# Who gets which 8 KB buffer in the last pass: a store ring of five, and all other buffers for loads

## The chip, the cores and the metric

The kernel runs on one core of a Trainium2 chip. The metric is the device time of one execution in microseconds, the median of several runs. Lower is better.

## The reference, cut to what matters

The reference computes four layers on one token and the gradients of all weights and of both caches by reverse differentiation. Layer A is attention over a cache of 65,536 positions with 32 query heads and 4 key/value heads; layer B is a dense layer with a squared ReLU. Both are used twice, with the same weights and the same cache.

```python
def A(x, k_cache, v_cache, wq, wo):          # Hq=32, Hkv=4, Dh=128, Sk=65536, D=1024
    q = (x @ wq) split into 32 heads
    scores = einsum("bhqd,bhkd->bhqk", q, repeat(k_cache, 8)) * Dh ** -0.5
    p = softmax(scores)
    return einsum("bhqk,bhkd->bhqd", p, repeat(v_cache, 8)) as one row @ wo
def B(x, w1, b1, w2, b2):
    return relu(x @ w1 + b1) ** 2 @ w2 + b2
x = x + A(layernorm(x)); x = x + B(layernorm(x))
x = x + A(layernorm(x)); x = x + B(layernorm(x))
# outputs: x, and the gradients of x, k_cache, v_cache, wq, wo, w1, b1, w2, b2 for a given grad_out
```

K and V caches are 64 MB each in bf16, and so are their two gradients. They make nearly all the traffic.

## The kernel before, in words

**Passes.** The caches don't fit on the chip, so they are read again in each of four passes: the two attention layers forward (`attn_fwd`, twice), the backward pass of the second attention layer (`attn_bwd3`), and the last pass (`attn_bwd4`, line 1263), which finishes the backward pass of the first attention layer and writes the gradients of K and V for both layers together. Dense stages lie between the passes.

**Buffers.** One tile, the arena (line 259), holds 20 buffers of 8 KB per partition, 1 MB each. Eight of them begin the last pass as planes that keep the softmax numerators of both attention layers for the four key/value groups; `E_done` (line 881) gives back the two planes of a group when that group is finished. Seven more begin it with V blocks that the pass before left there, already transposed. Five are free. Every other use takes a buffer by `take_one` (line 283) through `Slot` (line 305) and gives it back through `give_slot` (line 318). Taking and giving happen in the program's order, when the program is written, not at run time. `NOW["step"]` counts the steps of the pipeline, and `FREE` holds for each free buffer the step at which it was given back; a buffer that was handed to a store gets 5 steps added (`STORE_STEPS`, line 67). At run time, whoever overwrites a buffer waits by semaphore until its last use has ended: a matmul that reads it, or the DMA that stores it.

**The last pass.** Blocks are 32 cache rows per partition, 1 MB: 64 K blocks and 64 V blocks. Items are an eighth of a row group (8 columns); there are 256, and a step of `pipeline` (line 825) advances each stage by one. The stages, with their lags, stand in line 1439:

- `vT` (line 1311) loads a V block, transposes it on TensorE (line 1319) and copies it out of PSUM (line 1322); `vS` (line 1339) multiplies it with the output gradients (line 1350) and makes X on VectorE (line 1367).
- `eIn` (line 1325) copies the planes on GpSimd (line 1328); `eT` and `xT` transpose (line 1334) into `xt` (line 1336).
- `dV8` and `dK8` call `outer16` (line 1382), which takes a buffer (line 1385), fills it with the gradient of one half block in two steps (matmuls in line 1390, copies out of PSUM through `evac`, lines 161 on ScalarE and 164 on VectorE) and stores it (line 1396).
- `k8` (line 1409) loads a K block and multiplies it with X (line 1421).

Beside it runs a list of background work (`Background`, line 762): wo slabs for the output gradients of the next group and wq slabs for the input gradient (`slabs`, line 430, loaded in line 447, used by VectorE in line 583), and the weight gradients as outer products (`g_outer`, line 1492; `g_outer_wide`, line 1511; `g_outer_last`, line 1470), each of which fills a buffer named og over four calls and stores it (lines 1507, 1528, 1488).

**Queues.** All loads are issued by SyncE (SP) from one queue in order: cache blocks of this pass in line 350, weight slabs in line 447. A load whose buffer is still in use makes the queue wait, and all later loads with it. All stores are issued by GpSimd, in order with its copies. The first three passes are written under a manual schedule; the last is not, so a scheduler places its instructions on each engine.

**Which buffer is taken, before.** In the last pass a load takes, of the free buffers given back at least 9 steps ago (`AHEAD`, line 72), the newest, and if there is none the oldest free one (lines 289 to 293). What is filled by an engine takes, of those given back at least one step ago, the newest (lines 294 to 296). Weight slabs take the oldest (line 298). Some early K and V loads are issued by hand from a list, `nexts` (lines 1354 to 1357), and take the newest of all.

Of the kernel before, what the change touches and what calls it, by code (L numbers as in the profile page):

```python
# [20 lines left out]
def kernel(  # L21
# [47 lines left out]
    NSLOT = 12  # L69
    NWT = 6  # L70
    NKEEP = [8, 7, 7]
    AHEAD = 9

    const = ctx.enter_context(tc.tile_pool(name="const", bufs=1))
    vec = ctx.enter_context(tc.tile_pool(name="vec", bufs=1))
# [6 lines left out]
    PS = {}  # L82
# [8 lines left out]
    def ps_sc(shape, dtype=F32):  # L91
        return PS["pool"].tile(shape, dtype, name="ps_sc", tag="sc", bufs=1 if PS["pass4"] else 2)
# [47 lines left out]
    load = {"act": 0.0, "dve": 0.0, "pe": 0.0}  # L140
# [118 lines left out]
    ARENA = slotp.tile([P, NG * BLK], BF, name="arena")  # L259
    GRAN = [ARENA[:, i * BLK:(i + 1) * BLK] for i in range(NG)]  # L260
    FREE = {i: 0.0 for i in range(NG)}
    HELD, BUSY = set(), set()
    NOW = {"step": 0, "pairs": True, "wide": False, "newest": False}

    def wide(i):
        return ARENA[:, i * BLK:(i + 2) * BLK]
# [8 lines left out]
    def take_pair():  # L275
        both = [(max(FREE[i], FREE[i + 1]), i) for i in range(0, NG, 2) if i in FREE and i + 1 in FREE]
        if not both:
            return None
        i = min(both)[1]
        del FREE[i], FREE[i + 1]  # L280
        return i

    def take_one(fill, load=False):
        by_age = sorted((t, i) for i, t in FREE.items())
        if load and NOW["newest"]:
            i = by_age[-1][1]
            del FREE[i]
            return i
        if load and PS["pass4"]:
            early = [i for t, i in by_age if t <= NOW["step"] - AHEAD]  # L290
            i = early[-1] if early else by_age[0][1]
            del FREE[i]
            return i
        if fill:
            ready = [i for t, i in by_age if t <= NOW["step"] - 1]
            i = ready[-1] if ready else by_age[0][1]
        else:
            i = by_age[0][1]
        del FREE[i]
        return i  # L300

    def odd_one():
        return any((i ^ 1) not in FREE and t <= NOW["step"] - 16 for i, t in FREE.items())

    class Slot:
        def __init__(self, name, fill=False, at=None, both=False, load=False):
            self.i = take_one(fill, load) if at is None else at
            self.n = 2 if both else 1
            self.users, self.over = 0, False
            self.t = wide(self.i) if both else GRAN[self.i]  # L310
            BUSY.update(range(self.i, self.i + self.n))
# [6 lines left out]
    def give_slot(i, more=0):  # L318
        NOW["step"] += 0.01
        BUSY.discard(i)  # L320
        if i not in HELD:
            FREE[i] = NOW["step"] + more

    def kv_views(ap):
        return [ap[0, g].rearrange("(b p j) d -> b p j d", p=P, j=JW) for g in range(G)]
# [3 lines left out]
    def half(views, g, hb):  # L329
        return views[g][hb // 2][:, J * (hb % 2):J * (hb % 2) + J, :]  # L330
# [9 lines left out]
    def kv8(t, g, c8):  # L340
        hb, j = divmod(c8, J)
        key = (t, g, hb)
        have = KV["have"]
        if key not in have:
            i = None
            if NOW["pairs"] and hb % 2 == 0 and (t, g, hb + 1) not in have and key not in KV["halves"]:
                i = take_pair()
            if i is None:
                sl = Slot("blk_" + t, load=True)
                nc.sync.dma_start(out=sl.t.rearrange("p (j d) -> p j d", d=DH), in_=half(KVIN[t], g, hb))  # L350
                have[key] = sl
            else:
                for h in range(2):
                    have[(t, g, hb + h)] = Slot("blk_" + t, at=i + h)
                nc.sync.dma_start(out=wide(i).rearrange("p (j d) -> p j d", d=DH), in_=KVIN[t][g][hb // 2])
        return have[key].t.rearrange("p (j d) -> p j d", d=DH)[:, j:j + 8, :]
# [240 lines left out]
    class Rows:  # L597
        def __init__(self, pool=None, bufs=NWT):
            self.pool, self.bufs = pool, bufs
            self.views = deque()  # L600
            self.n = 0
            self.parts = 0
            if pool is None:

                for _ in range(2):
                    t = Slot("s_wt", True).t[:, :].rearrange("p (v a b) -> p v a b", v=4, a=8)
                    self.views.extend(t[:, v, :, :] for v in range(4))
                self.bufs = 8
            self.queue = deque()
            self.jobs = deque()  # L610
            self.feed = None
# [651 lines left out]
    def attn_bwd4(p, La, Lb, on_group, bg, stack, end=()):  # L1263
# [5 lines left out]
        state = {}  # L1269
# [7 lines left out]
        def g_setup(g):  # L1277
            sl = gsl(g)
            for i, L in enumerate((La, Lb)):
                nc.vector.tensor_copy(out=DOB[:, g, 0, i * R:(i + 1) * R], in_=L["dOT"][:, sl])  # L1280
                nc.vector.scalar_tensor_tensor(out=CCf[:, g, 0, i * R:(i + 1) * R], in0=L["qT"][:, sl], scalar=SCALE, in1=L["rZ"][:, sl],
                                               op0=ALU.mult, op1=ALU.mult)
                nc.vector.tensor_tensor(out=CCf[:, g, 1, i * R:(i + 1) * R], in0=L["dOT"][:, sl], in1=L["rZ"][:, sl], op=ALU.mult)
            ndt = dspool.tile([64, R2], BF, name="ndt4", tag="ndt4")
            for i, L in enumerate((La, Lb)):
                nc.vector.tensor_copy(out=ndt[:, i * R:(i + 1) * R], in_=L["nd2"][:, sl])
            state["ndt"] = ndt
# [51 lines left out]
        def vS(g, c8):  # L1339
            if c8 == gfirst[g]:  # L1340
                g_setup(g)
            vt = state.pop(("vt", g, c8))
            for i in range(8):
                s = (c8 + i) % J
                if s == 0:
                    state["ps_dp"] = ps_sc([P, J, R2])
                    nc.tensor.matmul(state["ps_dp"][:, :, :].rearrange("p c r -> p (c r)"), lhsT=sel2[:, :],  # L1347
                                     rhs=state["ndt"][:, :].unsqueeze(1).to_broadcast([64, J, R2]), start=True, stop=False)
                w = min(4, J - s)
                nc.tensor.matmul(state["ps_dp"][:, s:s + w, :].rearrange("p a b -> p (a b)"), lhsT=vt[:, i, :],  # L1350
                                 rhs=DOB[:, g, 0:w, :].rearrange("p a b -> p (a b)"), start=False, stop=(s == J - 1))
            if is_turned("v", g, c8):
                kv_done("v", g, c8)
                if c8 % J == J - 8 and nexts:
                    NOW["newest"] = True
                    kv8(*nexts.popleft())
                    NOW["newest"] = False
            if (c8 + 8) % J == 0:
                c0 = c8 + 8 - J
                ps_dp = state["ps_dp"]  # L1360
                if g == items[0][0]:
                    if c8 == J - 8 + items[0][1]:
                        state["Xs"] = Slot("xs", True)
                    X = state["Xs"].t.rearrange("p (n j r) -> p n j r", j=J, r=R2)[:, c0 // J % 8, :, :]
                else:
                    X = dspool.tile([P, J, R2], BF, name="X", tag="X", bufs=3)
                nc.vector.tensor_tensor(out=split2(X[:, :, :]), in0=split2(ps_dp[:, :, :]), in1=E2(g, c0, J), op=ALU.mult)
                add_load(dve=0.13 + J * R2 * 0.00105)
                state[("X", g, c0 // J)] = X
# [62 lines left out]
        start_pass(p)  # L1432
        for b in range(2):
            kv8("k", *items[b * J // 8])
        nexts = deque()
        for b in range(V_LEAD * 8 // J // 2):
            nexts.append(("k",) + items[(b + 2) * J // 8])
# [72 lines left out]

    def g_outer_wide(pool, out_dram, nA, nB, a_cols, b_cols):

        rsl = Slot("rowbw", True)
        rb = rsl.t
        for k in range(0, nB, 8):
            rows2(b_cols, (k, k + 4) if k + 4 < nB else (k,), rb[0:66, k * 64:k * 64 + 512], f=True)
            yield
        for a in range(nA):
            if a % 4 == 0:
                ra = pool.tile([66, 4 * P], BF, name="rowa", tag="rowa", bufs=2)  # L1520
                rows2(a_cols, (a, a), ra)
                yield
            sl = Slot("og", True)
            for k in range(0, nB, 8):
                rank2(sl.t[:, k * P:min(k + 8, nB) * P], lambda r: d_cols(ra[r, :], a % 4), lambda r: rb[r, k * 64:k * 64 + 512])
                if k + 8 < nB:
                    yield
            nc.gpsimd.dma_start(out=out_dram[a * P:(a + 1) * P, :], in_=sl.t[:, 0:nB * P])
            sl.free(stored=True)
            yield  # L1530
        rsl.free()
# [270 lines left out]
```

## Time and profile before

| what | value |
|---|---|
| runs | 2004.31, 2014.15, 2018.07 us, median 2014.15 |
| the profiled execution, span from first to last instruction | 2011.2 us (its own device time is not among the runs listed; the median lies 2.95 above the span) |
| TensorE busy, VectorE busy, ScalarE busy, GpSimd busy | 1627.2, 1171.7, 1045.1, 142.9 us |
| HBM read and written | 624.96 MB, 165.69 MB |
| mean rate over the span | 395 GB/s |
| the last pass, from 1230 to the end: moved, mean rate | 300.92 MB, 385 GB/s |
| stores of 1 MB from the arena, issue to landing, median | 10.4 us, 149 of them |

The page cuts the span into 40 slices of 50.3 us and gives for each the busy share of the engines and of the 16 DMA engines. Other views cut any stretch finer, say who waited for whom and for how long, and list for a line of the kernel its instructions and the time from issue to landing of its DMAs. A wait is put down to what ended last. "SPq" is the queue of DMA issues on SyncE, "PE" TensorE's matmuls, "PEld" its weight loads, "DVE" VectorE, "ACT" ScalarE, "POOL" GpSimd.

### The profile page before, as it was taken

The numbers are of one execution on the slowest core, as the hardware profiler recorded it, in microseconds if no ns is written. First come the engines' busy times: TensorE is split into PE (matmuls) and PEld (weight loads), VectorE is DVE, ScalarE is ACT, GpSimd is POOL, SyncE is SP. The second block draws the span as 40 slices with busy tenths as digits, with TensorE's granted clock in tenths as the row PEclk, the third lists the DMA queues.
The fourth block names the chain that finished last, engine by engine and source line by source line (L and its number), as shares of the span: only waits on it lengthen the run. The fifth ranks groups of instructions, "written<-read, shape, count | busy, mean of one in ns | idle before, by whom it ended". The sixth has DMA issues, their size and how long they took to land. (4 is left out here: it accounts for less than half of the span.)

```text
span 2011.2 us, 67084 instructions
## 1 busy us (share of the span) xinstructions
PE 1627.2 (81%) x30228; PEld 1319.5 (66%) x30228; DVE 1171.7 (58%) x2426; ACT 1045.1 (52%) x1608; POOL 142.9 (7%) x332
## 2 busy tenths in 40 slices
PE   6877788687877777878787888788789799977887
PEld 6877777687777776767777785455455465644554
DVE  5645555255545544435454477656677677866775
ACT  3534344253433453426354365656678576756765
POOL 0000000000000000000000001111111111111211
PEclk9989999699999998899888999878898877888996
DMA  9999999999999998899999987998999999999996
GB/s 390 421 424 420 424 424 402 395 405 420 425 420 424 425 391 335 356 421 424 417 420 412 394 311 284 360 377 350 394 418 424 423 411 370 418 423 388 424 404 243
DMA packets 101037, 794.98 MB, mean 395 GB/s; under 512 B 9472, under 2 KB 9486, under 8 KB 37134
## 3 DMA queue, kind: packets, MB, share of 16 engines
q1 hardware_dynamic: 76670, 624.99, 76.2%
q0 software_dynamic: 24080, 165.70, 20.0%
q8 instruction: 236, 3.87, 0.8%
q14 instruction: 51, 0.42, 0.1%
HBM read 624.96 MB, written 165.69 MB: 393 GB/s over the span
## 5 line engine op out<-in xcount | busy, mean ns | idle before, releaser
L164 DVE COPY kt<-ps_tr 128x1024 bf16<-128x1024 bf16 x724 | 496.4, 688 | 489.8 <-PE ps_tr L1007 252.6
L161 ACT CAST arena<-ps_gg 128x1024 bf16<-128x1024 f32 x457 | 446.9, 1012 | 234.2 <-PE ps_gg L1390 161.6
L1007 PE MATMUL ps_tr<-ident_b,arena 128*128 128x128 bf16 x3840 | 306.9, 224 | 45.6 <-DMA arena<-in_A_k_cache_dram 33.3
L161 ACT COPY kt<-ps_tr 128x1024 bf16<-128x1024 bf16 x164 | 170.9, 1047 | 191.7 <-PE ps_tr L1199 113.5
L1007 PEld LDWEIGHTS <-arena 128*128 128x128 bf16 x3840 | 231.4, 100 | 54.1 <-DMA arena<-in_A_k_cache_dram 36.5
L1109 PE MATMUL ps_acc<-arena 128*128 128x64 bf16 (+4 forms) x4096 | 203.8, 195 | 67.5 <-DMA arena<-in_A_v_cache_dram 53.8
L164 DVE CAST arena<-ps_gg 128x1024 bf16<-128x1024 f32 (+2 forms) x186 | 222.2, 1195 | 61.5 <-PE ps_gg L1390 32.4
L1390 PE MATMUL ps_gg<-GG,xt 64*128 64x512 bf16 x1024 | 221.5, 433 | 21.5 <-ACT arena L161 13.1
L1319 PE MATMUL ps_tr<-ident_b,arena 128*128 128x128 bf16 x1824 | 186.6, 240 | 39.1 <-DMA arena<-in_A_v_cache_dram 37.7
L1109 PEld LDWEIGHTS <-arena 128*128 128x128 bf16 x4096 | 157.7, 100 | 73.2 <-DMA arena<-in_A_v_cache_dram 57.4
L1090 ACT ACTIVATE arena<-S_sb,L_negm 128x128 bf16<-128x128 f32 x256 | 165.5, 1003 | 62.4 <-DVE L_negm L1075 62.4
L1199 PE MATMUL ps_tr<-ident_b,arena 128*128 128x128 bf16 x1920 | 157.9, 229 | 43.8 <-DMA arena<-in_A_v_cache_dram 41.6
L1025 PE MATMUL ps_sc<-L_qpad,kt 128*128 128x64 bf16 (+7 forms) x3584 | 181.7, 193 | 14.2 <-ACT kt L161 6.6
L1319 PEld LDWEIGHTS <-arena 128*128 128x128 bf16 x1824 | 123.9, 107 | 98.0 <-issue 56.1
L1025 PEld LDWEIGHTS <-kt 128*128 128x128 bf16 x3584 | 151.2, 100 | 19.3 <-ACT kt L161 8.9
L1199 PEld LDWEIGHTS <-arena 128*128 128x128 bf16 x1920 | 119.8, 103 | 49.3 <-DMA arena<-in_A_v_cache_dram 44.7
L1421 PEld LDWEIGHTS <-arena 128*128 128x128 bf16 x2048 | 97.8, 105 | 73.4 <-issue 47.5
L1090 ACT ACTIVATION_READ_ACCUMULATOR arena<-S_sb,L_negm 128x1 f32 x256 | 128.1, 500 | 0.0
L1350 PEld LDWEIGHTS <-kt 128*128 128x128 bf16 x1824 | 86.5, 104 | 56.6 <-issue 55.7
L1350 PE MATMUL ps_sc<-DOB,kt 128*128 128x64 bf16 (+3 forms) x1824 | 119.1, 201 | 0.0
L1244 PE MATMUL ps_acc<-dsT,arena 128*128 128x64 bf16 (+7 forms) x2048 | 103.8, 195 | 14.0 <-DMA arena<-in_A_k_cache_dram 10.4
L1421 PE MATMUL ps_acc<-X,arena 128*128 128x64 bf16 (+3 forms) x1536 | 99.6, 203 | 15.7 <-DMA arena<-in_A_k_cache_dram 15.7
(292 smaller groups left out, 2160.7 us busy)
## 6 DMA issues: line engine op xcount, KB each, us to landing
arena<-in_A_k_cache_dram SPq DMA_DIRECT2D x86, 2048.0 KB, 21.3
arena<-in_A_v_cache_dram SPq DMA_DIRECT2D x83, 2048.0 KB, 21.1
out_dram<-arena POOLq DMA_DIRECT2D x149, 1024.0 KB, 10.4
arena<-in_A_v_cache_dram SPq DMA_DIRECT2D x76, 1024.0 KB, 11.7
arena<-in_A_k_cache_dram SPq DMA_DIRECT2D x76, 1024.0 KB, 11.4
arena<-in_B_w_dram SPq DMA_DIRECT2D x32, 896.0 KB, 7.9
arena<-in_A_wo_dram SPq DMA_DIRECT2D x22, 1024.0 KB, 13.6
arena<-in_A_wq_dram SPq DMA_DIRECT2D x20, 1024.0 KB, 14.5
```

The lines of the kernel that those rows point to most:

```text
L161: nc.scalar.copy(out=out, in_=in_)
L164: nc.vector.tensor_copy(out=out, in_=in_)
L1007: nc.tensor.transpose(pt[:, i, :], kb8[:, i, :], ident_b[:, :])
L1025: nc.tensor.matmul(state["ps_s"][:, s:s + w, :].rearrange("p a b -> p (a b)"), lhsT=kt[:, i, :], rhs=L["qpad"][:, g, 0:w, :].rearrange("p ...
L1090: nc.scalar.activation(out=E(p, g, c0, SU)[:, :, h], in_=S[:, h, :], func=ACTF.Exp, bias=L["negm"][:, g, su, h:h + 1], scale=SCALE, accum_ ...
L1109: nc.tensor.matmul(ps_o[:, 0:w, :], lhsT=vb8[:, i, :], rhs=E(p, g, c, w), start=(c % SU == 0), stop=(c % SU == SU - 1), skip_group_check=True)
L1199: nc.tensor.transpose(pt[:, i, :], vb8[:, i, :], ident_b[:, :])
L1244: nc.tensor.matmul(ps_dq[:, 0:w, :].rearrange("p a b -> p (a b)"), lhsT=kb8[:, i, :], rhs=dsT[:, s:s + w, :].rearrange("p a b -> p (a b)") ...
L1319: nc.tensor.transpose(pt[:, i, :], vb8[:, i, :], ident_b[:, :])
L1350: nc.tensor.matmul(state["ps_dp"][:, s:s + w, :].rearrange("p a b -> p (a b)"), lhsT=vt[:, i, :], rhs=DOB[:, g, 0:w, :].rearrange("p a b - ...
L1390: nc.tensor.matmul(pg[:, 512 * h:512 * h + 512], lhsT=xt[64 * h:64 * h + 64, j1 // 8 + m, :], rhs=gg[64 * h:64 * h + 64, :, :].rearrange(" ...
L1421: nc.tensor.matmul(ps_dq[:, 0:w, :].rearrange("p a b -> p (a b)"), lhsT=kb8[:, i, :], rhs=X[:, s:s + w, :].rearrange("p a b -> p (a b)"), ...
```

## The change

In the last pass five buffers, the ring, are taken by what is stored, and the others by what is loaded or only used on the chip. Within each kind the one given back first is taken first. If the ring has none free, a store's buffer is the oldest of the rest; if the rest has none, a load takes the newest of the ring. The ring starts with two buffers that are free after the first two K loads. Once the list `nexts` is empty, buffers that are given back join it until it has five. Three uses that are filled by engines and never stored (`s_wt`, `xs`, `rowbw`) are no longer marked as filled, and so count with the loads. `AHEAD` is gone. The early loads by hand stay as they are.

```diff
-    AHEAD = 9
+    NRING = 5
...
-        if load and PS["pass4"]:
-            early = [i for t, i in by_age if t <= NOW["step"] - AHEAD]
-            i = early[-1] if early else by_age[0][1]
+        if PS["pass4"]:
+            mine = [i for _, i in by_age if (i in RING) == fill]
+            i = mine[0] if mine else by_age[0][1] if fill else by_age[-1][1]
             del FREE[i]
             return i
...
         if i not in HELD:
             FREE[i] = NOW["step"] + more
+            if PS["pass4"] and NOW["ring"] and len(RING) < NRING:
+                RING.add(i)
...
-                    t = Slot("s_wt", True).t[:, :].rearrange("p (v a b) -> p v a b", v=4, a=8)
+                    t = Slot("s_wt").t[:, :].rearrange("p (v a b) -> p v a b", v=4, a=8)
...
                     kv8(*nexts.popleft())
                     NOW["newest"] = False
+                    NOW["ring"] = not nexts
...
-                        state["Xs"] = Slot("xs", True)
+                        state["Xs"] = Slot("xs")
...
         for b in range(2):
             kv8("k", *items[b * J // 8])
+        RING.update(sorted(FREE)[:2])
         nexts = deque()
...
-        rsl = Slot("rowbw", True)
+        rsl = Slot("rowbw")
```

More of the change, by code (lines that the diff above doesn't have):

```diff
@@ L261 @@
     FREE = {i: 0.0 for i in range(NG)}
-    HELD, BUSY = set(), set()
-    NOW = {"step": 0, "pairs": True, "wide": False, "newest": False}
+    HELD, BUSY, RING = set(), set(), set()
+    NOW = {"step": 0, "pairs": True, "wide": False, "newest": False, "ring": False}
     def wide(i):
```

## The prediction

> **What bounds the kernel now.** I read the page's forty slices first, then the table of 25 us stretches, then who waits for DMA, and at last the DMA queue that issues the loads.
>
> ```profile
> DMA  9999999999999998899999987998999999999996
> GB/s 390 421 424 420 424 424 402 395 405 420 425 420 424 425 391 335 356 421 424 417 420 412 394 311 284 360 377 350 394 418 424 423 411 370 418 423 388 424 404 243
> ```
>
> One slice is 50.3 us. The 16 DMA engines are full for nearly the whole span, so bytes bound the kernel, and no byte is added or removed. Only time in which DMA is not full can be won. The last pass starts near 1225 us (slice 25). The stretches below show DMA share in the column before GB/s; a full one reads 1.01.
>
> ```profile
> core 0: us, PE busy (x) PEld busy (x) DVE busy (x) ACT busy (x) POOL busy (x), PEclk, DMA share, GB/s
> 1225.00:1250.00 25.00, 20.53 (x280) 13.19 (x279) 17.28 (x30) 13.43 (x15) 5.13 (x10) 0.86 0.76 306
> ...
> 1275.00:1300.00 25.00, 15.96 (x179) 9.50 (x178) 18.71 (x28) 15.65 (x21) 3.29 (x7) 0.80 0.79 301
> ...
> 1350.00:1375.00 25.00, 23.40 (x238) 13.71 (x238) 15.64 (x33) 14.61 (x16) 3.90 (x7) 0.73 0.80 310
> ...
> 1525.00:1550.00 25.00, 23.37 (x334) 15.58 (x331) 23.30 (x35) 23.55 (x33) 5.75 (x12) 1.00 1.01 424
> ...
> 1675.00:1700.00 25.00, 24.85 (x261) 14.35 (x260) 16.89 (x28) 15.69 (x18) 4.43 (x9) 0.71 0.92 348
> ...
> 1975.00:2000.00 25.00, 22.73 (x227) 13.74 (x225) 15.59 (x35) 14.90 (x16) 3.07 (x5) 0.59 0.51 203
> ```
>
> Idle DMA time is 25 us times (1.01 minus the share), added over the stretches of that table: 6.3 us in 1225 to 1250, 14.0 us in 1275 to 1425 (shares .79, 1.00, .99, .80, .98, .94), 7.3 us in 1425 to 1975 (.97, .92, .94, .99, .94 where not full), and 18.2 us in the tail after 1975, when no load is left. That is 27.6 us ahead of the tail. It is all that a better order of transfers can win.
>
> Who waits for a landing in the last pass (us in total, times, longest):
>
> ```profile
> PE ps_tr L1319 <- DMA arena<-in_A_v_cache_dram: 37.7, 12, 8.9
> ...
> PE ps_acc L1421 <- DMA arena<-in_A_k_cache_dram: 23.7, 7, 5.8
> ...
> ACT arena L161 <- DMA out_dram<-arena: 20.2, 5, 5.2
> ...
> DVE mv_t L583 <- DMA arena<-in_A_wo_dram: 8.4, 1, 8.4
> ...
> DVE arena L164 <- DMA out_dram<-arena: 5.1, 2, 3.8
> ```
>
> Loads come late: 69.8 us of waits. Engines that fill a staging buffer wait little for an older store: 25.3 us. The reason for the late loads stands in SP's own queue, here from 1225 to 1425 us:
>
> ```profile
> SPq L350 <- DMA out_dram<-arena: 137.6, 22, 12.8
> SPq L447 <- DMA out_dram<-arena: 42.2, 3, 20.7
> ```
>
> SP stood 179.8 of 200 us waiting until a store had left the buffer that the next load is to overwrite. It is one queue in order: the wait of 20.7 us for a wo slab (line 447, issued at last at 1270.3 us) held the V and K loads behind it until 1272.9 and 1275.9. DVE's 8.4 us wait for that slab follows, then PE's, then no stores are made, and the stretch from 1275 shows DMA at 0.79.
>
> **The change part by part.** Which buffer is taken follows from the program's order and lines 283 to 300, so it can be counted. A step of the pipeline is 3.0 us: the matmuls of line 1421 run from 1226.7 us (step 27) to 1984.8 us for the last K block (step 279).
>
> *Loads (135 in the pass).* Before, 108 overwrite a buffer that a store reads; after, none does: each waits for the last use by an engine. In steps 42 to 63 the buffer was given back 6 to 9 steps before the load's place in the program (18 to 27 us), from step 75 on 8 to 16 (mostly 10 to 13), at the end 16 to 21. A load lands in 11.5 us (median), so SP can issue it early enough. The wo slab takes the buffer of the third K block, whose last matmul ends at 1253.3 us: 17.0 us before the 1270.3 of now, more than the 8.4 us waited. In the stretch 1275 to 1425 the waits for loads (24.3 us of PE, 8.4 of DVE) exceed the 14.0 us of idle DMA that they leave. I take 11 of the 14.0 as won, and keep 0 and 14.0 as ends. From 1425 to 1975 I take 3 of 7.3: near 1835 DVE waits 7.0 us for a wq slab, which goes, but from 1680 to 1685 PE is busy 5.0 of 5.0 us at a granted clock of 0.50, which no load cures. At the start, 1225 to 1250, buffers are the same up to step 30; the first V load could go at 1244.4 us (last read of the second K block) and went at 1249.6; of 6.3 us idle I take 1.
>
> *Staging buffers (160 takes: K and V gradients, og, the bias row).* Before, 37 of them follow a store, nearly all 6 or 7 steps after it was issued; the others follow a read. After, 155 follow a store: 40 at 4 or 5 steps, 22 at 6, 78 at 7, 15 at 8 or 9. This is the added wait. It stands on ACT and DVE, in line 161 or 164; behind it queue the copies out of PSUM for V (line 1322) and X (line 1336), then PE, which needs those PSUM buffers, then POOL, whose xin copy (line 1328) waits for PE and has stores behind it. Store landings, 1225 to 1425 and 1700 to 1965:
>
> ```profile
> DMA to landing us min/median/max: 4.4/8.6/12.0
> ...
> DMA to landing us min/median/max: 6.4/12.6/21.4
> ```
>
> Four or five steps are 12 to 15 us, seven are 21. Early nothing waits; late about a quarter of the forty short reuses should, some 10 waits of 2 us, so 20 us on ACT or DVE. The row now says worse: 7 waits in 37, 25.3 us, which times 155/37 is 106 us. What hides it: while the oldest of five buffers is still being stored, two or three younger stores and the loads are queued, so DMA stays full, and PE has 61.4 us of waits for loads to give up. I charge 2 us, with 0 and the scaled row as ends (priced under the rivals). If the cover were gone, the whole 20 us would count.
>
> *Three buffers that are not stored (xs, rowbw, s_wt)* move to the load side: three takes, no instruction more, nothing. Until the list of early loads is used up the ring grows from 2 to 5, with the same distances as now (4 to 5 steps, landings at most 12.0 us): nothing, covered by the early landings.
>
> *Order.* The last pass has no hand-written order, so the instructions are placed anew: the same instructions on every engine, but 101 of SP's 426 DMA rows stand elsewhere (by -5 to +24 places, the +24 a wq slab that was fetched far ahead), and 91 of POOL's 337 by up to 4 places, mostly xin copies against stores. A wq slab lands in 19.4 us and its buffer is free 13 steps (39 us) early, so nothing; a store behind an xin copy may be 0.6 us late or early, both ways, so nothing.
>
> *The tail.* The last K load can go when a V block read near step 259 is free; it now goes at 1952.9 us, just before the last V block is read from 1956.4 (step 256 or so). So the tail keeps its length. Loads with up to 21 steps of lead leave more stores for the end: I charge 1 us, ends -2 and +5.
>
> Sum on the profiled span: -11 - 3 - 1 + 2 + 1 = -12, so 2011.2 becomes 1999.2. The median of the runs, 2014.15, lies 2.95 above that span, and I put the forecast on the median: 2014.15 - 12 = 2002.
>
> [...] The row is the store landing above, 8.6 us while DMA had gaps and 12.6 when it was full. [...]
>
> **The rivals.**
> *The gaps stay for another reason.* PE is busy 19 to 25 of 25 us in most stretches and its clock falls to 0.71 in one that is not full; loads that come earlier would then only wait in the buffers. Against it: in 1275 to 1300 PE is busy 16.0 us. Gain 0: 2014.
> *All gaps go.* 27.6 us ahead of the tail, no new wait: 2014.15 - 27.6 = 1986.6. Against it: the gap at the start precedes the change's first free buffer.
> *Five buffers are too few, slower.* One mechanism: a fill waits on ACT or DVE for the store of five steps ago, and PE and the next stores with it. Scaling the row gives 106 - 25.3 = 81 us more waits, less the 69.8 us for loads that go: +11, 2025. If each of the forty short reuses waits the mean of now (25.3/7 = 3.6 us), 144 - 25.3 - 69.8 = +49, 2063. Middle: +30, 2044. It decides once a store takes longer than about 15 us from issue to landing for most of the pass; now only the late maximum, 21.4, and a quarter of the late ones do.
> *It doesn't do what it says.* Excluded by the count: no load follows a store.
>
> **How the numbers follow.** Most gaps go: 0.53, 2002, its own range 1992 to 2010. No gain: 0.20, 2014. All gaps go: 0.12, 1987. Five too few: 0.15, 2025 to 2063. Below 1988 lies about half of the third case (0.06), above 2036 most of the fourth (0.10), so the range is 1988 to 2036. The bound of 1% (about what a measurement of this kernel can tell from no change) is 20.1 us: faster means under 1994.0, that is the third case and a fifth of the first, 0.22; slower means over 2034.3, most of the last, 0.13; within it 0.65.
>
> **What would show it.** Right: the stretches 1275 to 1425 at 1.00 or more; SP waits on PE and DVE rather than on out_dram; waits of lines 1319 and 1421 for loads under 20 us in the pass; waits of lines 161 and 164 for out_dram between 20 and 60 us in a pass whose DMA is full. Wrong: those waits over 100 us with DMA under 0.95 in the middle of the pass; gaps that end in PE's own work; a tail longer than 40 us.

## The result, and the profile after

The changed kernel takes 1980.99 us (median of four runs, 1979.35 to 1987.22), the kernel before 2011.33 us (median of four; one run joined the three shown). The ratio is 0.985, with an interval of 0.983 to 0.988: it is faster by 23 to 35 us. The forecast was 2002 with a range from 1988 to 2036, so the change won more than twice what was forecast. The profiled execution after has a span of 1985.4 us (1987.22 us of device time, the slowest of the four runs) against 2011.2, which is 25.8 us less.

The page's slices after, 49.6 us each:

```profile
DMA  9999999999999998899999988999999999999996
GB/s 389 423 422 422 423 425 400 394 400 420 425 419 424 425 405 310 359 421 420 421 422 421 411 304 307 406 425 404 397 424 424 425 425 411 361 424 424 425 377 256
```

In the busy digits little has changed. In the GB/s row the slices behind the pass's start (position 25 on, counted from 0) read 406, 425, 404 and 397, where 360, 377, 350 and 394 stood. The stretches of 25 us in the first group of the pass show where that comes from:

```profile
1225.00:1250.00 25.00, 20.71 (x288) 13.27 (x287) 17.81 (x30) 13.87 (x15) 5.11 (x10) 0.86 0.86 330
...
1275.00:1300.00 25.00, 21.94 (x248) 13.61 (x244) 18.65 (x29) 14.53 (x19) 3.62 (x7) 0.73 1.01 425
1300.00:1325.00 25.00, 22.88 (x304) 14.39 (x303) 20.21 (x46) 18.86 (x20) 5.75 (x11) 1.00 1.01 425
...
1350.00:1375.00 25.00, 23.50 (x330) 15.13 (x327) 20.09 (x36) 19.18 (x21) 5.98 (x12) 0.99 1.00 387
```

The last three columns are the granted TensorE clock, DMA share and GB/s. The stretch from 1275 moved 425 GB/s; it was 301. The matmuls done in it rose from 179 to 248.

**Count the time in bytes.** The best stretches run at 424 to 425 GB/s, and both kernels move the same bytes. So the time that a stretch loses is its length less its bytes at 425 GB/s. Three long stretches, of before and then of after:

```profile
1225.00:1425.00 200.00, 158.42 (x1861) 97.28 (x1860) 129.61 (x234) 118.67 (x135) 32.94 (x63) 0.81 0.91 353
1425.00:1925.00 500.00, 430.29 (x5297) 269.27 (x5296) 352.96 (x623) 345.55 (x414) 86.91 (x164) 0.85 1.00 412
1925.00:2011.20 86.20, 72.59 (x890) 45.08 (x888) 56.96 (x110) 55.25 (x59) 15.31 (x25) 0.80 0.77 306
```

```profile
1225.00:1425.00 200.00, 162.01 (x2054) 102.26 (x2053) 139.23 (x253) 128.63 (x147) 35.65 (x68) 0.88 0.98 400
1425.00:1925.00 500.00, 430.44 (x5319) 269.85 (x5318) 359.61 (x630) 348.26 (x415) 87.53 (x166) 0.86 1.00 414
1925.00:1985.40 60.40, 48.40 (x676) 30.73 (x674) 43.08 (x86) 40.92 (x45) 11.68 (x19) 0.91 0.68 272
```

The first 200 us lost 33.9 us before (200 x (1 - 353/425)) and lose 11.8 after: 22.1 us won. The next 500 us give 15.3 and 12.9, so 2.4; the rest 24.1 and 21.7, so 2.4. That is 26.9 with these rounded rates, against 25.8 between the spans. The order of the K blocks says the same in another way: the first matmul on block 8 of the pass (counted from 0) comes 15.9 us earlier than before, on block 16, the first of the second group, 26.1 us, the last matmul on the last block 21.5, and the end 25.8. Nearly all that was won is won in the first 200 us, and then kept.

SP's queue from 1225 to 1425 us, which stood 179.8 us behind stores:

```profile
SPq L352 <- PE ps_tr L1321: 71.8, 11, 23.7
SPq L352 <- PE ps_acc L1424: 65.4, 14, 11.6
SPq L449 <- PE ps_sc L1352: 17.8, 1, 17.8
```

No line of that answer names out_dram. SP still waits most of the time, but now for the last matmul that reads the buffer: it is as early as the buffers allow. The waits for a landing in the pass:

```profile
ACT arena L161 <- DMA out_dram<-arena: 44.5, 24, 4.0
DVE arena L164 <- DMA out_dram<-arena: 25.0, 11, 4.9
...
PE ps_acc L1424 <- DMA arena<-in_A_k_cache_dram: 15.4, 5, 11.2
...
DVE X L1370 <- DMA arena<-in_A_wq_dram: 12.7, 1, 12.7
...
PE ps_tr L1321 <- DMA arena<-in_A_v_cache_dram: 8.3, 2, 5.1
...
DVE arena L198 <- DMA out_dram<-arena: 4.4, 1, 4.4
```

TensorE's waits for K and V blocks fell from 61.4 to 23.7 us. What fills the ring now waits 73.9 us for older stores (44.5 + 25.0 + 4.4), where it waited 25.3.

**TensorE's clock moved too.** In the clock record of the pass only 0.5 and 1.0 occur; the time at 0.5 fell from 266 to 197 us.

### The profile page after: what moved, and what is told of

It is laid out like the page before. It is cut to its first block, busy times and chain, and to the rows that moved or that the text cites. A ratio compares the mean times of both kernels' runs of the same rounds, so it can differ in the third digit from the quotient of the medians.

```text
span 1985.4 us, 67093 instructions
## 1 busy us (share of the span) xinstructions
PE 1614.0 (81%) x30228; PEld 1317.7 (66%) x30228; DVE 1174.4 (59%) x2426; ACT 1043.6 (53%) x1608; POOL 142.6 (7%) x332
## 5 line engine op out<-in xcount | busy, mean ns | idle before, releaser
L1393 PE MATMUL ps_gg<-GG,xt 64*128 64x512 bf16 x1024 | 215.2, 418 | 28.2 <-ACT arena L161 10.1
L1027 PE MATMUL ps_sc<-L_qpad,kt 128*128 128x64 bf16 (+7 forms) x3584 | 183.6, 194 | 11.2 <-issue 6.4
L1352 PE MATMUL ps_sc<-DOB,kt 128*128 128x64 bf16 (+3 forms) x1824 | 114.7, 200 | 0.0
L1393 PEld LDWEIGHTS <-xt 64*128 64x128 bf16 x1024 | 65.7, 94 | 71.5 <-issue 33.0
## 6 DMA issues: line engine op xcount, KB each, us to landing
arena<-in_A_wo_dram SPq DMA_DIRECT2D x22, 1024.0 KB, 19.4
```

The source lines that it names most:

```text
L1027: nc.tensor.matmul(state["ps_s"][:, s:s + w, :].rearrange("p a b -> p (a b)"), lhsT=kt[:, i, :], rhs=L["qpad"][:, g, 0:w, :].rearrange("p ...
L1393: nc.tensor.matmul(pg[:, 512 * h:512 * h + 512], lhsT=xt[64 * h:64 * h + 64, j1 // 8 + m, :], rhs=gg[64 * h:64 * h + 64, :, :].rearrange(" ...
```

## The experiments

"Store waits" are those of ACT and DVE for out_dram, "load waits" those of PE, DVE and ACT for a load, both over the last pass. "Lost" is counted in bytes as above, from 1225 us to the end. "At 0.5" is the time in the pass at half the granted clock. The kernel before was run beside every one of them, and the ratios are to those runs.

| kernel | median us | ratio [95%] | lost us | at 0.5, us | store waits | load waits |
|---|---|---|---|---|---|---|
| before | 2011.33 | 1 | 73.1 | 266 | 25.3 | 79.7 |
| after | 1980.99 | 0.985 [0.983, 0.988] | 47.0 | 197 | 73.9 | 36.4 |
| e1, first group only | 2014.23 | 1.003 [1.002, 1.005] | 74.0 | 246 | 34.5 | 62.9 |
| e2, later groups only | 2005.42 | 0.998 [0.997, 1.000] | 68.8 | 243 | 50.7 | 41.9 |
| e3, order of loads only | 2011.18 | 1.002 [1.000, 1.003] | 71.3 | 243 | 25.4 | 86.6 |
| e4, slabs only | 2012.36 | 1.001 [1.000, 1.003] | 71.9 | 252 | 11.5 | 90.0 |
| e5, ring of three | 2127.21 | 1.058 [1.055, 1.061] | 190.2 | 395 | 261.2 | 1.4 |
| e6, ring of six | 1987.89 | 0.988 [0.986, 0.991] | 49.5 | 212 | 61.3 | 50.0 |
| e7, ring, old order of loads | 1981.63 | 0.985 [0.983, 0.988] | 43.9 | 198 | 63.1 | 37.9 |
| e8, ring grows to eight | 1991.17 | 0.990 [0.988, 0.992] | 54.6 | 205 | 36.9 | 75.7 |
| e9, three groups of four | 1981.62 | 0.986 [0.984, 0.988] | 40.8 | 199 | 51.8 | 44.9 |
| e12, two groups of four | 1984.85 | 0.986 [0.984, 0.989] | 43.5 | 189 | 51.5 | 46.5 |
| e10, before, fewer matmuls | 2040.65 | 1.016 [1.014, 1.019] | 92.4 | 321 | 16.7 | 117.6 |
| e11, after, fewer matmuls | 1989.12 | 0.990 [0.988, 0.992] | 47.9 | 277 | 60.0 | 44.9 |
| e13, before, more matmuls | 2004.82 | 0.996 [0.995, 0.998] | 62.3 | 191 | 31.6 | 79.5 |
| e14, after, more matmuls | 1989.34 | 0.989 [0.986, 0.992] | 49.2 | 192 | 104.2 | 17.1 |

Theory A, after the result: the first group wins, because there are few buffers there and the loads stand behind stores.

### e1 and e2: the rule in a part of the pass

Both rules stand in the code, and a flag chooses. e1 begins with the new rule and goes back to the old one when the first of four groups ends; e2 does the reverse.

```diff
+        if load and PS["pass4"] and not NOW["kinds"]:
+            early = [i for t, i in by_age if t <= NOW["step"] - 9]
+            i = early[-1] if early else by_age[0][1]
+            del FREE[i]
+            return i
-        if PS["pass4"]:
+        if PS["pass4"] and NOW["kinds"]:
...
                 state["Xs"].free()
+                NOW["kinds"] = False
```

> The new rule up to the end of the first key/value group (step 91), the old rule after it. Theory A: the time is won where only 12 buffers serve loads and stores and SP's queue stands behind stores, so 1225 to 1425 us; counted in bytes against a full rate of 425 GB/s, before lost 33.8 us there and after 11.8, so this kernel takes 22 us off before, near 1989. Rival B: keeping loads and stores apart pays all through the pass, in proportion to its groups; then a quarter to a third of the 30 us, 8 to 10 us, near 2002.

> The old rule in the first group, the new rule (ring filled from the buffers given back from step 92 on) after it. Theory A: 5 us off before, near 2006: before lost 15.1 us between 1425 and 1925 us and after 10.4. Rival B: 20 us or more, 1991 or less.

e1 lost what it won: 2014.23, 1.003 [1.002, 1.005]. It had the gain: block 16 came 24.5 us early. At block 20 it was 12.0, at block 24 it was 0.9, at the end nothing. In e1 from 1390 to 1480 us, SP's queue, and then two stretches, one of 10 us and one of 100:

```profile
SPq L357 <- DMA out_dram<-arena: 49.8, 7, 11.9
SPq L454 <- DMA out_dram<-arena: 26.3, 3, 16.3
```

```profile
1405.00:1415.00 10.00, 9.88 (x102) 6.21 (x102) 6.22 (x9) 6.99 (x7) 1.68 (x3) 0.77 0.60 249
1425.00:1525.00 100.00, 80.48 (x946) 48.98 (x943) 68.39 (x120) 70.20 (x86) 15.54 (x30) 0.82 0.98 388
```

As soon as loads may take stored buffers again, SP stands 76.1 of 90 us behind stores, and no load is issued between 1392.6 and 1417.3 us. So the mechanism shows again where it was put back. Theory A's -22 fell as a sum, though: a lead won in the first group isn't safe until the loads have enough other buffers. e2 came out 4 us under before, near the 5 that theory A gave the later groups, but its interval reaches no change (0.998 [0.997, 1.000]); its first 200 us lost 32.7, nearly as before.

### e9 and e12: when going back is harmless

The same flag, switched back later: e12 after two groups, e9 after three. Of the 20 buffers 14 go round once one group's planes are given back, 16 after two, 18 after three.

```diff
+            if (g, c8) == items[2 * len(items) // G - 1]:
+                NOW["kinds"] = False
```

> As the first-group experiment, but the new rule holds for three of the four groups and the old rule for the last only. Theory G (going back to loads that follow stores costs once, wherever it is done: SP stands behind stores until the lead is used up, some 15 us, and the rest of the loss is the old rule's own): about 15 us given back of 30, near 1996. Rival H (under the old rule the lost time comes back in each stretch, in proportion): a quarter to a third given back, 7 to 10 us, near 1990.

> As the first-group and the three-groups experiments, with the new rule for two of the four groups. Three groups kept the whole gain, one kept none. Theory G2 (going back is dear only while few buffers are free: 14 after the first group, 16 after the second, 18 after the third; with few, SP stands behind stores at once): most is kept, 20 us or more off before. Rival H2 (the second and third group win on their own): half of the gain, 15 us off.

e9 gave back nothing (0.986 [0.984, 0.988]) and both theories of it missed. e12 kept nearly all (0.986 [0.984, 0.989]), as theory G2 had it. In e12, SP's queue and the stretches at the time in which e1 fell back:

```profile
SPq L357 <- PE ps_acc L1429: 44.7, 6, 12.0
SPq L357 <- PE ps_tr L1326: 29.2, 5, 18.7
```

```profile
1405.00:1415.00 10.00, 9.74 (x127) 6.32 (x126) 8.06 (x12) 8.33 (x10) 2.22 (x4) 1.00 1.01 425
1425.00:1525.00 100.00, 88.09 (x1142) 56.99 (x1143) 78.83 (x139) 79.12 (x100) 18.42 (x36) 0.93 1.01 424
```

So the rule by kinds matters over the first half of the pass, in which 12 or 14 buffers are in circulation, and little or nothing beyond. There SP stands behind stores without harm: from 1625 to 1925 us it does so for 264.6 of 300 us in e12 and for 263.4 in before, in the changed kernel for none, and the three move 404, 406 and 406 GB/s. A queue that waits for stores thus cost time here only where its loads then came too late. That the number of buffers decides it, and not another trait of the first two groups, is argued and not tested.

What e1 gave back isn't wholly explained: it lost 14.9 us less than before up to 1425 us (19.0), but 24.6 from there to 1925, where before lost 15.3, and 30.3 at the end, where before lost 24.1. Only the first 100 us of that, 8.7 lost, are shown above to be SP behind stores; the rest lies in single dips, whose cause stays open.

### e3, e4 and e7: kinds, or only the order, or one slab

e3 is the kernel before, with loads that take the oldest free buffer. e4 is the kernel before, with slabs that take the oldest buffer that was read, not stored. e7 is the changed kernel, with the old order of loads among the buffers outside the ring.

```diff
-            early = [i for t, i in by_age if t <= NOW["step"] - AHEAD]
-            i = early[-1] if early else by_age[0][1]
+            i = by_age[0][1]
```

```diff
...
-            i = by_age[0][1]
+            read = [i for t, i in by_age if i not in STORED and t <= NOW["step"] - 3] if PS["pass4"] else []
+            i = read[0] if read else by_age[0][1]
...
+            (STORED.add if more else STORED.discard)(i)
```

```diff
+            if load:
+                mine = [i for t, i in by_age if i in mine and t <= NOW["step"] - 9][::-1] or mine
```

> The kernel before, except that cache loads of the last pass take the oldest free buffer, not the newest of those given back 9 steps ago; stores and kinds as before, and 108 of 135 loads still follow a store. Theory A: within 5 us of before, since SP still waits for stores in the first group (same distances there). Rival C: the order in which buffers come free, with the longer lead for loads, is what wins; then 15 us or more off before.

> The kernel before, except that wo and wq slabs of the last pass take the oldest free buffer that was last read and not stored; cache loads and stores as before. In the first group 2 of 3 slabs then follow a read. Rival D: the 20.7 us for which SP stood before a wo slab set off the whole loss; then 12 us or more off before. Theory A: that wait is one of 25 in the stretch, the others stay, 4 us off, 2007.

> The changed kernel, but cache loads take, of the buffers outside the ring, the newest of those given back 9 steps ago (the old order), else the oldest; stores as changed. Loads follow a read 9 steps (27 us) ago throughout the later groups instead of 10 to 21. Theory A2: what wins is that loads don't follow stores; 27 us cover a landing of 17 us, so within 5 us of the changed kernel, -28 from before. Rival C2: the longer lead of the order in which buffers came free carries the gain; then 10 us or more over the changed kernel.

The order is worth nothing: e3 takes 1.002 [1.000, 1.003] of the time before and e7 is equal to the change (0.985 [0.983, 0.988]). The landing of 17 us in its expectation isn't shown by a run here: the loads of line 352 in the changed kernel took 20.2 us from issue to landing (median; 35.7 at most), against its lead of 27. In e3 SP still stands behind stores from 1225 to 1425 us:

```profile
SPq L349 <- DMA out_dram<-arena: 131.4, 22, 13.6
SPq L446 <- DMA out_dram<-arena: 34.5, 3, 20.6
```

e4 takes 1.001 [1.000, 1.003]. The slab that the prediction singled out goes at 1257.7 us there, not at 1270.3, and VectorE no longer waits 8.4 us for it; so the lateness of that slab isn't the cause alone. Other loads wait for their own stores, 184.7 us in all against 179.8:

```profile
SPq L352 <- DMA out_dram<-arena: 161.0, 25, 12.7
SPq L449 <- DMA out_dram<-arena: 23.7, 2, 20.4
```

The longest wait, 20.7 us in before, is still there (20.4): it belongs to the slab ahead of that one, and e4 leaves it in place, so it doesn't test rival D's number. The changed kernel speaks against it: that earlier slab goes at 1239.2 us there and at 1241.9 in before, so the change took only 2.7 us from its wait.

### e5, e6 and e8: the size of the ring

```diff
-    NRING = 5
+    NRING = 3
```

e6 has 6 there. e8 begins with five and grows to eight after the first group.

> The changed kernel with three buffers in the ring instead of five; 92 of 116 later fills follow a store of 3 steps ago or less, the rest of 4 or 5, that is 6 to 15 us against 13.5 us to landing. Theory A2 (waits for stores cost little as long as younger stores are queued, here only one or none): the waits of ScalarE and VectorE grow from 70 us to 400 us or more and the time by 30 us or more over the changed kernel, past before. Rival: what stores wait for is hidden whatever the ring, then within 10 us of the changed kernel.

> The changed kernel with six buffers in the ring; later fills follow a store of 7 to 9 steps ago (21 to 27 us), loads follow a read 8 to 20 steps ago, in the first group 5 to 9. Theory A2: the 70 us of waits for stores go to under 25 us, but they were hidden, so within 6 us of the changed kernel; in the first group loads come a step later. Rival F (five is too few and its waits count): 10 us or more below the changed kernel.

> The changed kernel, but the ring grows to eight when the first group ends and planes come free: later fills follow a store of 9 to 13 steps ago, loads a read of 5 to 13 steps ago (15 to 39 us). Theory A2: waits for stores fall under 15 us and nothing is won by it, since DMA was full; loads of 5 or 6 steps lead (16 of them) begin to wait; 0 to +6 us against the changed kernel. Rival F: the 70 us of waits for stores counted, then 8 us or more below it.

With three, the rival "too few" is there: 1.058 [1.055, 1.061]. Its waits in the pass and its middle stretch:

```profile
ACT arena L161 <- DMA out_dram<-arena: 185.0, 61, 10.0
...
DVE arena L164 <- DMA out_dram<-arena: 71.6, 27, 7.1
```

```profile
1425.00:1925.00 500.00, 390.70 (x4595) 245.55 (x4592) 304.69 (x537) 291.93 (x346) 73.43 (x140) 0.81 0.92 351
```

Hardly any engine waits for a load there (1.4 us), and DMA falls to 351 GB/s in stretches in which five buffers give 414. With six (0.988 [0.986, 0.991]) and with eight later (0.990 [0.988, 0.992]) the store waits fall to 61.3 and 36.9 us, the load waits rise to 50.0 and 75.7, and the time rises or stays. Rival F is refuted; theory A2 had the waits wrong in all three (400 or more for three buffers, under 25 and under 15 for the others) and the time of e8 somewhat too low; its times for e5 and e6 held. From three to five the store waits decide; beyond five the load waits grow and nothing more is won.

### e10 and e11: is it TensorE's work?

In both, line 1421 does two of its eight matmuls a step, so 1536 matmuls of the pass are left out.

```diff
-            for i in range(8):
+            for i in (0, 7):
```

> The kernel before with 1536 of the 2048 matmuls of line 1421 left out (the dq sums of the last pass are then of a quarter of the terms); all transfers and buffers as before. Theory P (between waits the pass is bound by TensorE at its lowered clock, and the waits for loads lower the clock): lighter work gives 10 us or more, below 2000. Theory S (SP stands behind stores whatever TensorE does): under 5 us.

> The changed kernel with the same 1536 matmuls of line 1424 left out. Theory P: the two light kernels lie within 15 us of each other, since both come near the bound of the transfers. Theory S: they stay 25 to 30 us apart.

Both theories missed. With less work the kernel before became slower, 1.016 [1.014, 1.019]; the changed kernel with less work took 1989.12. They lie 51.5 us apart, where the full kernels lie 30 apart. In e10:

```profile
1225.00:1425.00 200.00, 145.17 (x1405) 82.12 (x1404) 125.12 (x228) 114.98 (x131) 31.65 (x61) 0.76 0.89 344
```

PE is busy 145 of 200 us and its clock is 0.76, below the 0.81 of before. So the amount of matmul work is not the bound. One thing more differs: the scheduler placed the instructions of these kernels anew. It did so in e3 and e4 too, which moved by only 0.2 and 0.1%.

### e13 and e14: more work for TensorE

The reverse: 512 matmuls that add zeros to ps_dq, over the whole pass.

```diff
+                if i in (2, 5):
+                    nc.tensor.matmul(ps_dq[:, 0:w, :].rearrange("p a b -> p (a b)"), lhsT=kb8[:, i, :],
+                                     rhs=ZERO[:, 0:w, :].rearrange("p a b -> p (a b)"), start=False, stop=False, skip_group_check=True)
```

> The kernel before with 512 matmuls more beside those of line 1421 (two in eight, the same weights, a tile of zeros added into the same sums), transfers and buffers as before. Theory P2 (the pass is bound in turns by TensorE at half its clock, and a busier TensorE keeps its clock): under 266 us at half clock in the pass and 5 us or more won, though 512 matmuls take some 37 us of TensorE at 25 us for 341. Rival P1 (TensorE's plain work is a bound): 10 us or more lost. Rival S (SP's order alone): within 4 us of before.

> The changed kernel with the same 512 matmuls more. Theory P2: within 5 us of the changed kernel, since it has 197 us at half clock and less to win. Rival P1: 10 us or more over it. Rival S: within 4 us.

More work made the kernel before faster, 0.996 [0.995, 0.998], about 7 us. In e13:

```profile
1225.00:1425.00 200.00, 170.55 (x2132) 106.07 (x2130) 137.17 (x249) 129.54 (x148) 36.58 (x68) 0.84 0.95 373
```

The load waits are those of before (79.5 and 79.7 us) and SP stands as long behind stores; what changed is the time at half clock, 266 to 191 us, near that of the changed kernel (197). Theory P2's two figures hold for e13 (under 266 us, 5 us or more won). In the changed kernel the same addition left the clock where it was (192) and took some 7 us more: 0.989 [0.986, 0.992] beside 0.985 [0.983, 0.988], intervals that just overlap; P2 had it within 5. This speaks for the clock as a part of the gain. It isn't proof, since the traces show the instructions in another order here as well, and e3 and e4 moved by up to 0.2% with nothing but order and buffers changed. An estimate of the clock's part, from these two runs: 7 us net in e13, up to 15 if the added matmuls cost e13 the 7 that they cost e14. The rest, 15 to 23 of the 30, would be the early loads' own. Closer than that it isn't separated.

## Why the prediction was right, and where it was wrong

**The mechanism was right.** "After, none does": in the last pass no wait of SP ahead of a load names a store. The 1275 to 1425 stretches stand at 1.00 or more but for one at 0.96. The waits for loads of lines 1319 and 1421 were to be under 20 us in the pass and are 23.7: a sign narrowly missed, though three fifths less than 61.4.

**The term that was mis-sized is the first of the sum: 11 of 14.0 us of idle DMA time in 1275 to 1425.** In bytes these 150 us had lost 25.0 us, and lose 5.6 after: 19.4 won. By the prediction's own measure the term nearly came true, since by shares 1.5 us are left of the 14.0 and 12.5 went; the measure was wrong. The prediction read "idle" off the busy share. That share counts the time in which a DMA engine has a packet under way, however long the packet takes: the packet times of the queues from 1225 to 1425 us add up to 90.8% before (49.3 and 41.0 below, 0.5 for instructions), and the stretch shows 0.91. In the kernel before, this stretch was read as nearly full:

```profile
1300.00:1325.00 25.00, 21.44 (x177) 11.83 (x177) 11.19 (x29) 10.78 (x12) 3.37 (x6) 0.52 1.00 394
```

A share of 1.00, but 394 GB/s and not 425. The queues of 1225 to 1425 us (packets, MB, share of the 16 engines; q0 carries the stores, q1 the loads) tell where it goes, of before and then of after:

```profile
q0 software_dynamic: 5522, 40.26, 49.3%
q1 hardware_dynamic: 4120, 30.07, 41.0%
```

```profile
q0 software_dynamic: 5804, 42.31, 51.1%
q1 hardware_dynamic: 5122, 37.34, 46.7%
```

A load packet held an engine for 318 ns on average before (41.0% of 200 us x 16 engines, over 4120 packets) and for 292 after (46.7%, 5122), at the same mean size of 7.3 KB; a store packet 286 and 282. Not every packet took longer: in the records of the two traces the median of the full load packets (8 KB) is 309 ns in both, but 378 of 3671 took over 450 ns before and 202 of 4558 after. Why a packet takes that long isn't shown. The sum of the prediction with bytes in place of shares would have had 33.9 us to win by 1425 us, not 20.3; 1250 to 1275 us, which it counted as full, gave 1.2 (394 GB/s before, 415 after).

Of the 21 us between the forecast and the median, the sum accounts for 13.8 (12 foreseen, 25.8 between the profiled spans). The rest lies in the spread of the runs: the median of before came out at 2011.33 and not 2014.15, and the profiled execution after is the slowest of its four.

**Its own bound was counted in the same measure.** "That is 27.6 us ahead of the tail. It is all that a better order of transfers can win": up to 1925 us shares count 25.3 of them, bytes 49.2, of which the change won 24.5. Whether a better order can win more than 27.6 stays open: the most that a run here won up to 1925 us is about 27.5 (e6). The rival "All gaps go", 1986.6, came nearest in time, but that is luck, since it isn't what happened: gaps remain at the start (0.86, 330 GB/s) and near 1350 (387).

**The granted clock was taken as given.** "PE is busy 5.0 of 5.0 us at a granted clock of 0.50, which no load cures" may hold for its place, but not for the pass: between 1300 and 1325 PE's clock was 0.52 and is 1.00, with 304 matmuls where 177 stood. The clock there had fallen at 1300.5 us, in a wait of 3.7 us for a late K block. The time at half clock also moves without the change (e10 321 us, e13 191, before 266). The rival "The gaps stay for another reason" fell with the gaps.

**The added waits were mis-sized as well, at no cost.** About 20 us were foreseen, 10 waits of 2 us; 73.9 were measured, 36 waits of 2.05 us. So the number of waits was wrong, not their length. Lines 161 and 164 wait 69.5 us, beyond the 60 that the prediction's sign allowed. The landing itself, 12.0 us early (8.6 before), 14.6 (1425 to 1700 us) and 13.4 later, was longer than the prediction's row, 8.6 and 12.6. The cover held: DMA ran 414 GB/s from 1425 to 1925 us. The condition of the rival "Five buffers are too few", landings over 15 us for most of the pass, wasn't met: 53 of 160 took longer. e5 shows what happens without the cover: 261.2 us of such waits and 5.8%.

**Small terms, and a misreading.** From 1425 to 1975 the 3 us stand beside 2.4 measured to 1925. The reason given for them failed: the wait for a wq slab, "which goes", came back at another place as the 12.7 us of line 1370 above, which end at 1696.4 us, and 1675 to 1700 still shows 352 GB/s. The start gave 1.4 in 1225 to 1250 (7.0 lost, 5.6 after), where 1 was taken. The tail got no longer: the last matmul on a K block comes 21.5 us earlier and the end 25.8, where 1 us had been charged. The wait of 20.7 us isn't that of the slab issued at 1270.3 us, as the prediction has it: it ended at 1241.9 us, with the slab before, and the slab of 1270.3 had held SP for 11.2. That this slab could go 17.0 us sooner came true: it now goes at 1252.9.

## What to carry to other kernels

Where loads leave from one queue in order, ask what the first waiting load is waiting for: if it is a store, and the transfers run short there, keep what is stored and what is loaded in separate buffers, with just enough for the stores under way (here three cost 5.8%, five won 1.5%, six 1.2%). Size the gain by the bytes of the best stretch, not by the busy share, and look at stretches of 25 us, since a page's slices average it away. A lead won in one stage is kept only if the next stage can't lose it the same way (e1).

## What the runs showed of the hardware

**A busy TensorE can be one at half clock.** In the kernel before, between 1630 and 1645 us, with DMA full:

```profile
1630.00:1635.00 5.00, 5.00 (x42) 2.71 (x41) 3.87 (x6) 4.18 (x6) 0.53 (x1) 0.50 1.02 423
1635.00:1640.00 5.00, 5.00 (x54) 3.45 (x52) 2.51 (x5) 3.26 (x6) 0.00 (x0) 0.50 1.01 428
1640.00:1645.00 5.00, 5.00 (x47) 2.88 (x45) 4.22 (x5) 2.97 (x3) 1.69 (x3) 0.50 1.01 401
```

PE is busy in all 15 us and stays at 0.50. The costliest matmuls show the price, here in 1300 to 1325 us of before and after (the number between the comma and the last bar is the mean ns of one):

```profile
L1390 PE MATMUL ps_gg<-GG,xt 64*128 64x512 bf16 x24 | 6.6, 581 | 0.0
L1319 PE MATMUL ps_tr<-ident_b,arena 128*128 128x128 bf16 x40 | 5.9, 308 | 0.7 <-DMA arena<-in_A_v_cache_dram 0.7
```

```profile
L1393 PE MATMUL ps_gg<-GG,xt 64*128 64x512 bf16 x48 | 9.0, 381 | 1.7 <-DVE arena L164 1.3
L1321 PE MATMUL ps_tr<-ident_b,arena 128*128 128x128 bf16 x64 | 5.8, 220 | 0.0
```

581 against 381 ns and 308 against 220: at a granted clock of 0.52, the mean of the stretch, these two took 1.5 and 1.4 times as long as at 1.00. The clock record of the pass knows 0.5 and 1.0. In before the clock fell at 1276.6 us, 3.4 us into a PE wait of 7.9 us, but it also fell at 1628.2 us, ahead of the rows above, behind a wait of only 2.0 us. And 15 us of busy PE in these rows stay at half. What makes the clock fall or come back isn't shown by any run here.

**This kernel got faster with more matmuls and slower with fewer.** With 512 matmuls on zeros added it took 0.2 to 0.5% less (e13), and with 1536 left out 1.4 to 1.9% more (e10), though DMA was 0.95 busy from 1225 us to the end of before. The time at half clock moved the same way (191 us in e13 and 321 in e10, 266 before). That the clock is the reason isn't shown, since the order of the instructions differs too.
